# Half packs between score runs, finished input chunks as tile room, and seven instead of four quads with more VectorE exponentials

## The chip, the cores and the metric

The kernel runs on one core of a Trainium2 chip. The metric is the device time of one execution in microseconds (us). The runs of one call are repeated on one chip, and each call for a comparison times the kernel before as well. The profile's span is some 1.6 to 2.7 us shorter than the time of the same execution.

## The reference

Sequence 2048, width 512, 32 heads of 16. An attention branch and a gated bilinear branch on the same input are mixed by one sigmoid per row:

```python
g = _sigmoid((x * gate_w).sum(-1, keepdims=True))
a = _A_ref(x, A_wqkv, A_wo)      # softmax attention, 32 heads of 16
b = _B_ref(x, B_w_gate, B_w_up, B_w_down)   # (x Wg) * (x Wu), then Wd; F = 1376
return g * a + (1 - g) * b
```

The costly part is 32 heads x 2048 x 2048 exponentials.

## The kernel before

The Python program is a planner. It keeps a clock for each engine, and at each step decides what that engine issues next, from durations that are written into it. What comes out is a fixed order of instructions with semaphores; the chip then runs that order, at its own pace. So nearly every constant in the source changes the order and not an instruction.

The work is cut into 32 "quads" (4 row groups of the array, one chunk of 512 queries). Each quad has 64 score tiles of 128 x 512. TensorE makes up to four of them in one run. Their exponentials come in two ways:

```python
# ScalarE: two or three tiles (banks of PSUM) in one instruction
src = bass.AP(lo.tensor, lo.offset, [list(lo.ap[0]), [1, 512 * n]])
k = _Task("act", [sc] + old,
    lambda a: a.activation(cell_ap(c), src, ACT.Exp, scale=LN2 / 128.0),
    AOH + 0.4267 * n, ...)

# VectorE ("D" unit): integer arithmetic on the bits, one tile, then three shifted copies
lambda v: v.tensor_scalar(cell_ap(..., int16), bk.ap, CB, 0.0, ALU.add, ALU.max)
fn = lambda v: v.tensor_single_scalar(cell_ap(c, I16), cell_ap(src, I16), 32.0 * k, ALU.add)
# [the copies are shared between VectorE and GpSimd]
```

A ScalarE tile is used in one weighted product, a VectorE tile in four (itself and three copies, with weights scaled). 16 of the 64 tiles of a quad go to VectorE; in the quads listed in `HBQ` it is 20:

```python
HBQ = [16, 22, 24, 30]
UA0.append(UA0[-1] + (44 if m in HBQ else 48))   # tiles of ScalarE in a quad
```

Between score runs TensorE does the weighted products and the "fills", all other matrix products, in packs of 512 columns. A score run uses another tiling mode than these. The planner lets a pack go first only if the scores would still be in time:

```python
tN = act_need()          # when ScalarE will have emptied its queue
tL = tN - 0.62
...
if ua == 0 or (can and t + PACK > max(tE, tL) + 0.08):
    return False         # [wait for the score run: the pack does not fit]
```

If VectorE's tiles lag by more than `LC`, one is handed back to ScalarE (`convert()`).

The softmax here doesn't subtract the row's maximum and nothing guards it: scores larger than these inputs give would overflow.

## Time and profile before

| | before |
|---|---|
| median time | 712.44 us |
| first exponential starts, from the start of the span | 8.8 us |
| exponentials, first start to last end | 691.4 us |
| tail after the last exponential | 9.8 us |
| ScalarE tiles, in instructions | 1520, in 671 |
| VectorE tiles | 528 |

The prediction below shows the lines. In them, psS and psX are buffers in PSUM, the memory to which TensorE writes its results; PT, wv, wd, hT and xT hold finished exponentials (the last four are buffers whose first content nobody reads any more).

In the tables below, "bubbles" are the sum, over all exponentials, of what each ended later after the one before it than 0.490, 0.917 or 1.343 us (one, two or three tiles). The kernel before has 0.4 us of them.

### The profile page before, as it was taken

What the parts mean: (1) busy time and instruction counts of PE and PEld (TensorE: products, weight loads), DVE (VectorE), ACT (ScalarE), POOL (GpSimd) and SP (SyncE); (2) the same over time, 40 slices, a digit from 0 to 9 for tenths busy, and PEclk for the clock granted to TensorE, in tenths of its full rate; (3) what the DMA queues carried; (4) which work ended last, traced back from release to release, by engine and by line L of the source; (5) the groups of instructions that cost most, each with busy time, mean ns of one, the idle gap of its engine ahead of it and who ended that gap; (6) DMA issues with size and microseconds to landing.
All of it is one profiled execution on the core that took longest, in us unless ns stands there. A gap on an engine that the chain in (4) does not pass through costs nothing.

```text
span 710.0 us, 21364 instructions
## 1 busy us (share of the span) xinstructions
PE 688.3 (97%) x9127; PEld 188.7 (27%) x9127; DVE 644.5 (91%) x1231; ACT 696.6 (98%) x686; POOL 459.3 (65%) x481
## 2 busy tenths in 40 slices
PE   8999999999999999999999999999999999999997
PEld 3323332222222222222222222222222222222222
DVE  6998999999998999898999989999899999988897
ACT  6999999999999999999999999999999999999995
POOL 4787788746654566575577565556768866665863
PEclk9999999999999999999999999999999999999999
DMA  6800001000200000000001010000000001000001
GB/s 141 258 10 11 20 19 22 17 18 22 82 21 17 18 29 26 20 18 20 18 2 28 25 44 17 17 7 18 20 18 18 21 18 36 18 20 18 8 16 46
DMA packets 33055, 21.66 MB, mean 31 GB/s; under 512 B 20380, under 2 KB 27964, under 8 KB 32960
## 3 DMA queue, kind: packets, MB, share of 16 engines
q1 hardware_dynamic: 31632, 19.64, 9.5%
q8 instruction: 71, 1.16, 0.7%
q10 hardware_dynamic: 1328, 0.66, 0.4%
q14 instruction: 24, 0.20, 0.1%
HBM read 15.12 MB, written 2.36 MB: 25 GB/s over the span
## 4 chain that ended last, share of the span: by engine, by line
ACT 70%; PE 22%; DVE 3%; issue 3%; POOL 1%; DVEq 0%; POOLq 0%; ACTq 0%
ACT PT L1697 59%; PE psS L494 8%; PE psO L1226 6%; PE psX L563 5%; ACT wd L1697 5%; ACT wv L1697 4%; ACT hT L1697 2%; DVE PT L1083 1%; PE psS L563 1%; POOL PT L1164 1%; DVE PT L1161 1%; PE psX L494 1%; PE psO L1805 0%; DVE wk L898 0%; PE psS L1816 0%
## 5 line engine op out<-in xcount | busy, mean ns | idle before, releaser
L1697 ACT ACTIVATE PT<-psS 128x1024 bf16<-128x1024 f32 (+1 forms) x569 | 621.9, 1466 | 0.1
L1164 POOL TENSOR_SCALAR PT<-PT 128x1024 int16<-128x1024 int16 x233 | 250.5, 1084 | 134.9 <-DVE PT L1161 46.3
L494 PE MATMUL psS<-QM,KE 32*128 32x512 bf16 x1981 | 253.9, 375 | 11.4 <-ACT PT L1697 4.5
L1083 DVE TENSOR_SCALAR PT<-psS 128x512 int16<-128x512 f32 x349 | 237.2, 686 | 26.9 <-PE psS L494 24.0
L1226 PE MATMUL psO<-PT,VS 128*18 128x512 bf16 x1698 | 225.3, 381 | 1.0 <-DVE oraw L1255 1.0
L1226 PE MATMUL psO<-PT,VD 128*18 128x512 bf16 x1228 | 194.9, 381 | 0.0
L1024 PEld LDWEIGHTS <-KE 32*128 32x128 bf16 x2048 | 63.2, 91 | 278.2 <-issue 159.1
L1161 DVE TENSOR_SCALAR PT<-PT 128x1024 int16<-128x1024 int16 (+1 forms) x240 | 102.4, 455 | 1.0
L1164 POOL TENSOR_SCALAR PT<-wv 128x1024 int16<-128x1024 int16 x57 | 60.7, 1075 | 32.7 <-DVE wv L1083 14.0
L1226 PEld LDWEIGHTS psO<-PT,VS 128*18 128x18 bf16 x1698 | 53.5, 88 | 52.0 <-issue 35.5
L1697 ACT ACTIVATE wv<-psS 128x1024 bf16<-128x1024 f32 (+1 forms) x48 | 67.0, 1395 | 0.0
L563 PE MATMUL psX<-wd,hT 128*32 128x512 bf16 (+1 forms) x704 | 59.8, 386 | 0.0
L1226 PEld LDWEIGHTS psO<-PT,VD 128*18 128x18 bf16 x1228 | 46.4, 88 | 35.2 <-issue 24.5
L1083 DVE TENSOR_SCALAR wv<-psS 128x512 int16<-128x512 f32 x71 | 48.3, 687 | 7.0 <-PE psS L494 6.7
L563 PE MATMUL psX<-xT,wu 128*32 128x512 bf16 x688 | 53.8, 384 | 0.0
L563 PE MATMUL psX<-xT,wg 128*32 128x512 bf16 x688 | 53.6, 383 | 0.0
L1226 PE MATMUL psO<-wv,VS 128*18 128x512 bf16 x179 | 51.4, 381 | 0.0
L1697 ACT ACTIVATE wd<-psS 128x1024 bf16<-128x1024 f32 (+1 forms) x37 | 47.6, 1411 | 0.0
L1226 PE MATMUL psO<-wv,VD 128*18 128x512 bf16 x174 | 39.4, 381 | 0.2 <-ACT PT L1697 0.2
L1164 POOL TENSOR_SCALAR wv<-PT 128x1024 int16<-128x1024 int16 x23 | 24.9, 1082 | 22.4 <-PE psO L1226 9.0
L1083 DVE TENSOR_SCALAR PT<-psX 128x512 int16<-128x512 f32 x49 | 33.7, 688 | 5.7 <-PE psS L494 5.1
L837 DVE TENSOR_TENSOR hT<-psX,usb 128x512 bf16<-128x512 f32 (+1 forms) x44 | 30.1, 683 | 2.4 <-PE psX L563 1.7
(128 smaller groups left out, 715.8 us busy)
## 6 DMA issues: line engine op xcount, KB each, us to landing
rb<-rscr SPq DMA_DIRECT2D x31, 256.0 KB
out_dram<-ost SPq DMA_DIRECT2D x12, 128.0 KB, 1.7
wu<-in_B_w_up_dram SPq DMA_DIRECT2D x1, 1376.0 KB, 8.0
wg<-in_B_w_gate_dram SPq DMA_DIRECT2D x1, 1376.0 KB, 11.0
wd<-in_B_w_down_dram SPq DMA_DIRECT2D x1, 1280.0 KB, 6.0
OT<-OX SPq DMA_DIRECT2D x60, 16.0 KB, 1.8
wo<-in_A_wo_dram SPq DMA_DIRECT2D x1, 512.0 KB, 11.6
out_dram<-wk SPq DMA_DIRECT2D x4, 128.0 KB, 1.7
```

The costliest lines, as they stand in the source:

```text
L494: return e.add_instruction(mybir.InstMatmult(name=nc.get_next_instruction_name(), engine=mybir.EngineType.PE, ins=[e.lower_ap(rhs), e.lowe ...
L563: return e.matmul(out_ap[32 * q : 32 * q + w, :], lhs[:, 32 * q : 32 * q + w], rhs, start=s0, stop=s1, tile_position=(0, 32 * q), skip_gro ...
L837: lambda v: v.tensor_tensor(hT[0:w, f, :], bk.ap[0:w, :], usb[0:w, n % 2, :], ALU.mult),
L1024: r = e.ldweights(w, tile_position=pos)
L1083: lambda v: v.tensor_scalar(cell_ap(pr["cell"][i : i + 1], mybir.dt.int16), bk.ap, CB, 0.0, ALU.add, ALU.max),
L1161: fn = lambda v: v.tensor_single_scalar(cell_ap(c, I16), cell_ap(src, I16), 32.0 * k, ALU.add)
L1164: fn = lambda g: g.tensor_scalar(cell_ap(c, I16), cell_ap(src, I16), 32.0 * k, 1.0, ALU.add, ALU.mult)
L1226: r = e.matmul(psO[32 * j : 32 * j + VW, :], pv_stationary(m, kt, j, k), cell_ap((cell,)), start=s0, stop=s1, tile_position=(0, 32 * j), s ...
L1697: lambda a: a.activation(cell_ap(c), src, ACT.Exp, scale=LN2 / 128.0),
```

## The change

Its intent: to take more exponentials from ScalarE (seven quads for four), and to make room for the work that this gives TensorE, with fill packs that can be split in two and with room for tiles in parts of the input that nobody reads any more. Some twenty constants of the planner are changed with it. The core of the diff, with cuts marked:

```diff
-    HBQ = [16, 22, 24, 30]
+    HBQ = [6, 9, 14, 16, 22, 24, 30]
...
+        for i in range(16):
+            cells[C_X + i].need = 10**6 if i in XNO else 3 * NB + 1 + 2 * FT
...
-        groups = [(C_H, FT, EH), (C_D, FT, ED), (C_V, 4, 9999), (0, NMAIN, 9999)]
+        groups = [(C_H, FT, EH), (C_D, FT, ED), (C_X, 16, 9999), (C_V, 4, 9999), (0, NMAIN, 9999)]
...
+        HP = 1
+        HPK = 0.112
...
         def col(out_ap, lhs, rhs, s0, s1):
+            if hsel[0] is not None:
+                hs = slice(256 * hsel[0], 256 * hsel[0] + 256)
+                out_ap = out_ap[:, hs]
+                rhs = rhs[:, hs]
...
-            if ua == 0 or (can and t + PACK > max(tE, tL) + 0.08):
+            if ua == 0:
                 return False
+            if can and t + PACK > max(tE, tN - TL2) + TLS:
+                return half_pack(t, max(tE, tN - TL2) + TLS - HTL)
...
-        LC = 7
-        LDO = 8
+        LC = 5
+        LDO = 6
+        TLM = 0.62
+        TLS = 0.08
+        TL2 = 0.7
...
-        AOH = 0.057
+        AOH = 0.0635
[cut: F0, WP, GP, PB, KW, LAP, LAC, CPR, LA2, FB, NFD, QMW, RSV, and the switch costs SW, SWC, PCX]
```

More of the change, by code (lines that the diff above doesn't have):

```diff
@@ L213, in _build @@
     C_V = NMAIN
-    C_H = C_V + 4
+    C_X = C_V + 4
+    C_H = C_X + 16
     C_D = C_H + FT
@@ L410, in _build @@
         flex = [slots[0][2], slots[1][2], X]
+        XNO = (0, 4)
         cells = [_Cell() for _ in range(NCELL)]
-        for i in range(C_V, C_H):
+        for i in range(C_V, C_X):
             cells[i].need = NB * NCH
+        for i in range(16):
+            cells[C_X + i].need = 10**6 if i in XNO else 3 * NB + 1 + 2 * FT
         for i in range(C_H, C_D):
@@ L418, in cell_ap @@
         def cell_ap(c, dt=None):
-            for buf, lo in ((wd, C_D), (hT, C_H), (wv, C_V), (PT, 0)):
+            for buf, lo in ((wd, C_D), (hT, C_H), (xT, C_X), (wv, C_V), (PT, 0)):
                 if c[0] >= lo:
@@ L422, in cell_ap @@
             w = 512
-            base = buf[:, c[0] - lo, :]
+            base = buf[:, (c[0] - lo) // 4, (c[0] - lo) % 4 * 512 : (c[0] - lo) % 4 * 512 + 512] if buf is xT else buf[:, c[0] - lo, :]
             dims = [[1, 512]]
@@ L484, in _build @@
         LKD = -0.07
+        HP = 1
+        HPK = 0.112
+        HTL = 0.04
         LKP = 0.1
         QMP = 3.2
-        QMW = 0.3
+        QMW = 0.0
         PLAT = 0.44
-        SW = 0.11
+        SW = 0.1035
+        SWC = 0.0945
+        PCX = 0.005
         pe = {"mode": "c"}
@@ L508, in pe_run @@
         def pe_run(deps, fn, occ, mode, t, lat=None, cb=None, pre=None):
-            sw = SW if mode != pe["mode"] else 0.0
+            sw = (SW if mode == "r" else SWC) if mode != pe["mode"] else 0.0
+            if mode == "c" and occ == PACK:
+                occ += PCX
             pe["mode"] = mode
@@ L548, in __init__ @@
                 self.pdeps = None
+                self.h = 0
         def fready(f, t):
@@ L558, in xdep @@
             return xt_all if ch == 0 else [d_x[ch]]
+        hsel = [None]
         def col(out_ap, lhs, rhs, s0, s1):
+            if hsel[0] is not None:
+                hs = slice(256 * hsel[0], 256 * hsel[0] + 256)
+                out_ap = out_ap[:, hs]
+                rhs = rhs[:, hs]
             def fn(e, q):
@@ L1103, in even @@
         def even(c):
-            g = [sum(x >= lo for lo in (C_V, C_H, C_D)) for x in c]
+            g = [sum(x >= lo for lo in (C_V, C_X, C_H, C_D)) for x in c]
             return min(g) == max(g) and c[1] > c[0] and all(b - a == c[1] - c[0] for a, b in zip(c, c[1:]))
@@ L1321, in _build @@
         HWF = 0.2
-        GP = 200.0
+        GP = 190.0
         K3L = 190
@@ L1333, in _build @@
                 fills.append(f_q(0, b, pos) if kind == "q" else f_k(b, ch, pos) if kind == "k" else f_v(b, ch, pos))
-        F0 = 210.0
-        WP = 36.0
+        F0 = 220.0
+        WP = 28.0
         WL = 18.0
@@ L1407, in start_fill, with do_fill @@
             st["fill"] = f
-        def do_fill(t):
+        def do_fill(t, half=False):
             f = st["fill"]
             mk, occ, mode = f.packs[f.i]
-            deps = f.old + f.deps() if f.i == 0 else []
+            deps = f.old + f.deps() if f.i == 0 and not f.h else []
             if f.pdeps is not None:
                 deps = deps + f.pdeps[f.i]
-            k = pe_run(deps, mk(f.bank), occ, mode, t)
+            if half or f.h:
+                hsel[0] = f.h
+                occ = HPK
+            fn = mk(f.bank)
+            hsel[0] = None
+            k = pe_run(deps, fn, occ, mode, t)
+            if occ == HPK and not f.h:
+                f.h = 1
+                HN[0] += 1
+                return k
+            f.h = 0
             f.i += 1
@@ L1421, in do_fill @@
                 if f.name[0] == "v":
-                    for i in range(C_V, C_H):
+                    for i in range(C_V, C_X):
                         cells[i].readers.append(k)
+                ch = {"k": f.name[-1], "q": f.name[1:2], "g": f.name[1:2], "u": f.name[1:2], "v": str(int(f.name[-1]) // 2) if f.name[0] == "v" else ""}.get(f.name[0], "")
+                for i in range(16):
+                    if f.name == "gate" or ch == str(i % 4):
+                        cells[C_X + i].readers.append(k)
                 st["fill"] = None
@@ L1443, in _build @@
         LEAD = 5
-        PB = 0.45
+        PB = 0.4
         PK = 2
-        KW = 4.0
-        LAP = 0.12
-        LAC = 0.1
-        CPR = 3.5
-        LC = 7
-        LDO = 8
+        KW = 4.5
+        LAP = 0.08
+        LAC = 0.12
+        CPR = 3.1
+        LC = 5
[3 more added lines that the diff above has]
+        TL2 = 0.7
         MG = 0.15
@@ L1458, in _build @@
         LA1 = 1
-        LA2 = 99
+        LA2 = 3
         XF = -99
-        FB = 0
+        FB = 3
         SWE = 0
-        NFD = 20
-        AOH = 0.057
+        NFD = 24
+        AOH = 0.0635
         M4 = 1
@@ L1469, in _build @@
         DEV = 0.6
-        RSV = 0.5
+        RSV = 0.0
         RSC = 1.0
@@ L1512, in convert, with half_pack @@
             st["na"] += 1
+        HN = [0]
+        def half_pack(t, lim):
+            f = st["fill"]
+            if f is None or f.name[0] not in "kqudw" + ("g" if f.name != "gate" else "") or t + HPK > lim or not HP or st["ua"] < 20:
+                return False
+            do_fill(t, not f.h)
+            return True
         def pe_step():
@@ L1528, in pe_step @@
             tN = act_need()
-            tL = tN - 0.62
+            tL = tN - TLM
             if can and tE <= t + (SWE if pe["mode"] != "r" else 0.0):
@@ L1541, in pe_step @@
                             return True
-                    return False
+                    return half_pack(t, tL - MG + 0.1)
                 fw = fill_next(t) if st["fill"] is None else None
@@ L1618, in run_at @@
             if len(exps) < 2 and all(f is not None for f in fr):
-                return max(max(fr) + SEM, act_need() - 0.62 - MG)
+                return max(max(fr) + SEM, act_need() - TLM - MG)
             if not exps:
@@ L1940, in _build @@
         _build.end = max(clock.values())
+        _build.hn = HN[0]
         now("sp", [o_out[T - 1], o_out[T - 2]], lambda e: e.nop(), 0.1)
```

## The prediction

> **What bounds the kernel now.** I read the page first, then the groups of instructions by shape on ScalarE, the time order of ScalarE, the waits, the stretches of 100 us, and at last the time order of TensorE. The page alone does not decide it: TensorE, VectorE and ScalarE all stand above 90%.
>
> ```profile
> PE 688.3 (97%) x9127; PEld 188.7 (27%) x9127; DVE 644.5 (91%) x1231; ACT 696.6 (98%) x686; POOL 459.3 (65%) x481
> ACT 70%; PE 22%; DVE 3%; issue 3%; POOL 1%; DVEq 0%; POOLq 0%; ACTq 0%
> ```
>
> The groups by shape count the exponential tiles (128x512 each) that ScalarE makes, two or three to an instruction:
>
> ```profile
> L1697 ACT ACTIVATE PT<-psS 128x1024 bf16<-128x1024 f32 x405 | 444.8, 1343 | 0.1
> L1697 ACT ACTIVATE PT<-psS 128x1536 bf16<-128x1536 f32 x163 | 285.4, 1775 | 0.0
> L1697 ACT ACTIVATE wv<-psS 128x1024 bf16<-128x1024 f32 x43 | 58.1, 1352 | 0.0
> L1697 ACT ACTIVATE wd<-psS 128x1024 bf16<-128x1024 f32 x28 | 33.8, 1295 | 0.0
> L1697 ACT ACTIVATE hT<-psS 128x1024 bf16<-128x1024 f32 x15 | 17.5, 1251 | 0.2 <-PE psS L494 0.2
> ```
>
> With the three smaller rows of 1536 columns (9, 5, 2) and one of 512 these are 491 two-tile, 179 three-tile and 1 one-tile instructions: 671 instructions, 982 + 537 + 1 = 1520 tiles. The kernel has 2048 score tiles; the other 528 are exponentials by integer arithmetic on VectorE (its rows at L1083 sum to 528). 1520 is exactly 32 quads of 48 less 4 for each of the four listed quads, so no tile was handed back from VectorE to ScalarE.
>
> The durations of 1.34 and 1.78 us overlap, so they are not the price. The time order gives it:
>
> ```profile
> 174.19 1.79 ACT L1697 ACTIVATE PT<-psS 128x1536 bf16<-128x1536 f32 x1
> 175.54 1.36 ACT L1697 ACTIVATE wd<-psS 128x1024 bf16<-128x1024 f32 x1
> 176.46 1.36 ACT L1697 ACTIVATE PT<-psS 128x1024 bf16<-128x1024 f32 x1
> 177.38 1.78 ACT L1697 ACTIVATE wd<-psS 128x1536 bf16<-128x1536 f32 x1
> ...
> 694.71 5.46 ACT L1697 ACTIVATE PT<-psS 128x1024 bf16<-128x1024 f32 x5
> 702.64 0.28 ACT L1922 ACTIVATE oraw<-psS 128x128 f32<-128x128 f32 x1 [2.48 <-PE psS L563]
> ```
>
> End to end: 175.98, 176.90, 177.82, 179.16. A two-tile instruction takes 0.92 us, a three-tile one 1.34 us; in the records 0.917 and 1.343, almost without spread. So a tile costs 0.426 us and an instruction 0.065 us besides. Check: the first exponential ends at 9.81, and 9.81 + 490 x 0.917 + 179 x 1.343 + 0.49 = 700.1; the last line above ends at 700.17. From 8.8 to 700.2 us ScalarE has **no bubble at all**. The wait view agrees: the only wait before an exponential is the first one's 0.2 us. What is left is a head of 8.8 us and a tail of 9.8 us.
>
> TensorE at 97% is not the bound: its ends are modelled and its record runs on while it waits. In its time order a score run is followed by products and then a return to scores:
>
> ```profile
> 41.65 0.39 PE L1226 MATMUL psO<-PT,VD 128*18 128x512 bf16 x4
> 42.03 0.37 PE L494 MATMUL psS<-QM,KE 32*128 32x512 bf16 x2
> 42.33 0.40 PE L563 MATMUL psS<-xT,wk 128*32 128x512 bf16 x4
> 42.56 0.39 PE L1226 MATMUL psO<-PT,VD 128*18 128x512 bf16 x4
> 42.95 0.37 PE L494 MATMUL psS<-QM,KE 32*128 32x512 bf16 x2
> ```
>
> Pack to pack is 0.22 us, score to pack 0.30, pack to score 0.38 here (42.03 - 41.65). Over all 670 returns in the records the last step has a mean of 0.385 and a smallest regular value of 0.32. The difference, 0.065 x 670 = some 43 us, is time in which a whole pack of 512 columns did not fit. And scores are early: in half of the runs they start 0.05 us after ScalarE frees their banks, and end 0.49 us before ScalarE has to have them.
>
> **What the Trainium skill says.** "ScalarE: Activation LUTs", section What ACT_TABLE_LOAD costs: 0.833 ns a column, a fixed part, and back-to-back instructions overlap by some 93 ns. The slope agrees (0.426 us for 512 columns); what remains fixed here is 0.065 us. "TensorE: Matmul & The Clock Gate", Back-to-back issue gap: N/2.4 + 2.5 ns, which is 109 ns for 256 columns. This kernel already has such packs (V projections): 24 matmuls, four at a time, are on record for 0.84 us where four alone take 0.28, so (0.84 - 0.28)/5 = 0.112 us a pack. "TensorEngine Tiling (Array Packing)", Key Properties: changing the tiling mode drains the array. It agrees: both 0.30 and 0.32 exceed a 0.216 us pack by a change of mode.
>
> **The change, part by part.**
> (1) Seven listed quads, not four. Each moves four tiles from ScalarE to VectorE: 3 x 4 = 12 tiles, 1520 to 1508 and 528 to 540. On the path: -12 x 0.426 = **-5.1 us**. Beside it: VectorE gets 12 evacuations at 0.60 (7.2 us; 0.69 as recorded, 0.60 end to end) and 36 shifted copies, shared with GpSimd as before (some 19 tiles at 0.17 and 17 at 0.54, 3 and 9 us). VectorE idles 65 us and GpSimd 250 us of the span. TensorE gets 36 more weighted products (a VectorE tile takes four instead of one): 9 packs x 0.216 = 1.9 us. The new quads belong to the same two head blocks, so no table of weights grows.
> (2) Half packs. A fill pack may be split in two of 256 columns where the gap holds no whole one. Cost: 0.224 for 0.216 us of work, nothing on the path; gain: perhaps a hundred to two hundred of the gaps used, 11 to 22 us of the 43. It removes no work from ScalarE, so alone it is worth nothing here; it pays for (1).
> (3) Finished chunks of xT as 14 more tile cells, only after a chunk's last reader, so from about 40% of the span on. No exponential waits for a cell now, so worth 0 by itself.
> (4) New scheduling constants. Scores are allowed to come a little earlier (0.70 for 0.62), the assumed ScalarE overhead and switch costs are nearer to the measured ones: worth 0 where there are no bubbles. Score runs may take a VectorE tile also into the other slot's third bank: slightly more full runs, fewer and larger ScalarE instructions. I guess 4 fewer of 671, -0.3 us. Against that, the lag at which a VectorE tile is handed back is 5 for 7: each costs 0.43 us; I guess two, +0.9 us. Some first bubbles: +0.2 us, a guess.
> Sum: 712.4 - 5.1 - 0.3 + 0.9 + 0.2 = 708.1; head and tail as they are. Since the constants look chosen to make the new plan pay, I lean on fewer returned tiles and put **707.3 us**.
>
> **The rivals.**
> A. VectorE becomes the limit in the listed quads: tiles lag, are handed back, and most of the 12 return to ScalarE. For: 91% busy, more than 20 us of waits on scores that cannot be moved, a lower hand-back limit. Against: no hand-back before, 65 us idle. It would give 710 to 712.
> B. TensorE becomes late: half packs and 9 more packs push score runs past the moment at which ScalarE runs dry. For: starts of the runs are already up to 0.42 us behind the release. Against: a reserve of 0.49 us, and 43 us of gaps for 2 us of new work. With 0.1 us in each of 30 runs it takes back 3 us: 709 to 711; badly out of step it could pass 714.
> C. The half packs clear the backlog and shorten the tail (9.8 us), or the fuller runs save more instructions: 704.5 to 706. Against: the tail is a serial chain after the last product; its longest wait, 2.5 us on ScalarE, is for the last quad's sums, not backlog.
>
> **Range and chances.** Full transfer and small gains give 705; half of the tiles handed back or some bubbles give 710. 8 in 10: 704.8 to 710.6. Faster by 2% means below 698.1: 14 us, where the only term on the path is 5. Slower by 2% (726.6) needs a stall of a kind that the trace does not show. Chances: faster 0.02, within 2% 0.95, slower 0.03.
>
> **What would show it.** Right: ScalarE tiles sum to 1508 to 1512 and VectorE's L1083 rows to 540 or a little less; exponentials still 0.917 and 1.343 us apart without waits; the last one ends near 695; matmul rows of 256 columns for the fills, with more matmuls in all; pack-to-score gaps nearer to 0.32. Wrong: waits of ScalarE on L494 (rival B), 1515 tiles or more (A), or a tail much shorter than 9.8 us (C). It would be wrong altogether if the end moved by more than the count of ScalarE tiles explains.

## The result

The changed kernel takes 707.29 us (706.72 to 707.46, 4 runs) against 712.44 us (711.67 to 712.72, 4 runs): -5.15 us. The ratio is 0.9928, 95% interval 0.9911 to 0.9945. Here and below a ratio is the mean time of one kernel's runs over that of the other's in the same rounds, so it is not quite the ratio of the medians.

The page of the changed kernel, engines and chain:

```profile
PE 682.9 (97%) x9299; PEld 193.8 (27%) x9299; DVE 651.9 (92%) x1223; ACT 691.7 (98%) x685; POOL 499.6 (71%) x515
ACT 71%; PE 22%; DVE 4%; issue 2%; POOL 0%; DVEq 0%; ACTq 0%; POOLq 0%
```

Hardly a share has moved, and that is right: the bound is the same engine, only with less to do. Its groups by shape, the two-tile ones and the largest three-tile one:

```profile
L1744 ACT ACTIVATE PT<-psS 128x1024 bf16<-128x1024 f32 x350 | 384.1, 1298 | 0.1
L1744 ACT ACTIVATE PT<-psS 128x1536 bf16<-128x1536 f32 x152 | 257.6, 1727 | 0.0
L1744 ACT ACTIVATE wv<-psS 128x1024 bf16<-128x1024 f32 x51 | 65.3, 1280 | 0.1
L1744 ACT ACTIVATE xT<-psS 128x1024 bf16<-128x1024 f32 x49 | 62.6, 1293 | 0.0
L1744 ACT ACTIVATE wd<-psS 128x1024 bf16<-128x1024 f32 x33 | 38.0, 1235 | 0.0
L1744 ACT ACTIVATE hT<-psS 128x1024 bf16<-128x1024 f32 x17 | 19.8, 1206 | 0.2 <-PE psS L503 0.2
```

These are 500 two-tile instructions. With 169 of three tiles (152, and 7, 6, 3, 1 in rows not shown) and one of one tile they make 670 instructions and 1000 + 507 + 1 = 1508 tiles. None was handed back, and VectorE has 540 (the sum of its rows at L1102). The end in the time order of ScalarE:

```profile
692.51 1.77 ACT L1744 ACTIVATE PT<-psS 128x1536 bf16<-128x1536 f32 x1
693.84 2.27 ACT L1744 ACTIVATE xT<-psS 128x1536 bf16<-128x1536 f32 x2
698.05 0.28 ACT L1969 ACTIVATE oraw<-psS 128x128 f32<-128x128 f32 x1 [1.93 <-PE psS L582]
```

The last exponential ends at 693.84 + 2.27 = 696.11. The first one starts at 9.56, so this stretch is 686.6 us long, 4.8 us less than before. That is 12 x 0.426 + 1 x 0.065 = 5.2 us less work and 0.4 us more bubbles (0.7 for 0.4). The head was 0.8 us longer in this execution (over all profiled ones it lay between 8.5 and 9.6 us, whatever the kernel). The tail is 705.4 - 696.1 = 9.3 us, 0.5 us shorter.

The split packs are the matmul rows of 256 columns at L582. I show the two largest:

```profile
L582 PE MATMUL psX<-wd,hT 128*32 128x256 bf16 x136 | 9.8, 278 | 0.0
L582 PE MATMUL psX<-xT,wu 128*32 128x256 bf16 x40 | 2.9, 278 | 0.0
```

All such rows together hold 272 matmuls, eight to a split pack: **34 packs** were split, of more than 700.

So the sum came out. The prediction also said why the parts matter: the quads pay, the half packs make room for them. That is what the experiments test.

### The profile page after: what moved, and what is told of

It is laid out like the page before. It is cut to its first block, busy times and chain, and to the rows that moved or that the text cites. A ratio compares the mean times of both kernels' runs of the same rounds, so it can differ in the third digit from the quotient of the medians.

```text
span 705.4 us, 21702 instructions
## 1 busy us (share of the span) xinstructions
PE 682.9 (97%) x9299; PEld 193.8 (27%) x9299; DVE 651.9 (92%) x1223; ACT 691.7 (98%) x685; POOL 499.6 (71%) x515
## 4 chain that ended last, share of the span: by engine, by line
ACT 71%; PE 22%; DVE 4%; issue 2%; POOL 0%; DVEq 0%; ACTq 0%; POOLq 0%
ACT PT L1744 55%; PE psS L503 7%; ACT xT L1744 7%; PE psO L1245 6%; ACT wv L1744 5%; PE psX L582 5%; ACT wd L1744 2%; ACT hT L1744 2%; PE psS L582 1%; PE psX L503 1%; DVE PT L1102 1%; PE psS L693 1%; PE psX L693 1%; PE psO L1852 0%; DVE PT L1180 0%
## 5 line engine op out<-in xcount | busy, mean ns | idle before, releaser
L1744 ACT ACTIVATE PT<-psS 128x1024 bf16<-128x1024 f32 (+1 forms) x502 | 568.1, 1428 | 0.1
L1183 POOL TENSOR_SCALAR PT<-PT 128x1024 int16<-128x1024 int16 x183 | 198.4, 1094 | 82.3 <-DVE PT L1102 31.8
L1102 DVE TENSOR_SCALAR PT<-psS 128x512 int16<-128x512 f32 x292 | 197.4, 684 | 14.0 <-PE psS L503 11.7
L1744 ACT ACTIVATE xT<-psS 128x1024 bf16<-128x1024 f32 (+2 forms) x56 | 72.8, 1338 | 0.0
L1180 DVE TENSOR_SCALAR PT<-PT 128x1024 int16<-128x1024 int16 x141 | 66.9, 491 | 0.8 <-PE psO L1245 0.2
L1183 POOL TENSOR_SCALAR PT<-xT 128x1024 int16<-128x1024 int16 x46 | 50.3, 1099 | 24.0 <-DVE xT L1102 7.9
L1102 DVE TENSOR_SCALAR xT<-psS 128x512 int16<-128x512 f32 x76 | 51.6, 686 | 6.2 <-PE psS L503 5.9
L582 PE MATMUL psX<-wd,hT 128*32 128x512 bf16 (+3 forms) x784 | 55.9, 362 | 0.0
L582 PE MATMUL psX<-xT,wu 128*32 128x512 bf16 (+1 forms) x708 | 55.1, 378 | 0.3 <-DVE ost L917 0.3
L582 PE MATMUL psX<-xT,wg 128*32 128x512 bf16 (+1 forms) x696 | 54.3, 381 | 0.4 <-DVE KE L621 0.4
L1245 PE MATMUL psO<-xT,VS 128*18 128x512 bf16 x203 | 51.4, 381 | 0.7 <-DVE oraw L1274 0.4
L1245 PE MATMUL psO<-xT,VD 128*18 128x512 bf16 x242 | 51.1, 380 | 0.1
L1183 POOL TENSOR_SCALAR PT<-wv 128x1024 int16<-128x1024 int16 x34 | 36.8, 1089 | 9.1 <-DVE PT L1180 2.8
L1102 DVE TENSOR_SCALAR PT<-psX 128x512 int16<-128x512 f32 x52 | 35.7, 686 | 6.1 <-PE psS L503 5.5
```

What stands on the lines that cost most here:

```text
L582: return e.matmul(out_ap[32 * q : 32 * q + w, :], lhs[:, 32 * q : 32 * q + w], rhs, start=s0, stop=s1, tile_position=(0, 32 * q), skip_gro ...
L1102: lambda v: v.tensor_scalar(cell_ap(pr["cell"][i : i + 1], mybir.dt.int16), bk.ap, CB, 0.0, ALU.add, ALU.max),
L1183: fn = lambda g: g.tensor_scalar(cell_ap(c, I16), cell_ap(src, I16), 32.0 * k, 1.0, ALU.add, ALU.mult)
L1245: r = e.matmul(psO[32 * j : 32 * j + VW, :], pv_stationary(m, kt, j, k), cell_ap((cell,)), start=s0, stop=s1, tile_position=(0, 32 * j), s ...
```

## The experiments

Two kinds are told apart. In one the order of the instructions is left as it is and the length of some work is changed. In the other the planner makes a new order, and then everything moves. "Replanned" marks the second kind. One table for all; tiles, instructions, bubbles and tail are from the profiled execution of each.

| run | time (median) | ratio to before | ScalarE tiles in instructions | bubbles | tail |
|---|---|---|---|---|---|
| before | 712.44 | 1 | 1520 in 671 | 0.4 | 9.8 |
| changed | 707.29 | 0.9928 | 1508 in 670 | 0.7 | 9.3 |
| b_cut12 | 708.06 | 0.9944 | 1508 in 671 | 1.8 | 9.8 |
| b_pe44 | 712.74 | 1.0011 | 1520 in 671 | 0.6 | 9.8 |
| a_cut24 | 701.30 | 0.9845 | 1484 in 670 | 5.7 | 9.3 |
| a_pe44 | 707.36 | 0.9932 | 1508 in 670 | 1.5 | 9.2 |
| a_whole34 | 707.04 | 0.9923 | 1508 in 670 | 1.3 | 9.2 |
| a_no_half (replanned) | 730.91 | 1.0264 | 1510 in 712 | 4.3 | 26.5 |
| a_no_half_tuned (replanned) | 708.81 | 0.9951 | 1508 in 658 | 4.0 | 9.1 |
| a_no_cells (replanned) | 708.47 | 0.9948 | 1508 in 672 | 1.2 | 10.7 |
| a_four (replanned) | 714.05 | 1.0029 | 1520 in 659 | 3.6 | 9.4 |
| b_six (replanned) | 717.41 | 1.0067 | 1512 in 689 | 0.6 | 17.4 |
| nine (replanned) | 704.41 | 0.9891 | 1500 in 666 | 2.8 | 9.0 |
| nine_no_half (replanned) | 707.13 | 0.9929 | 1500 in 668 | 7.5 | 9.1 |

Not all of these bubbles come from the order. In five of the runs the trace shows TensorE's granted clock at 0.5 for some microseconds while exponentials are still being made (`--windows`, column PEclk). In the other nine it is below 1 only after the last exponential.

| run | half clock, us from the start of the span | bubbles there or within about 1 us after | all bubbles | mean clock, all executions |
|---|---|---|---|---|
| a_cut24 | 678.7-682.1 | 1.1 | 5.7 | 0.997 in the profiled one, 1.0 in three |
| a_no_half_tuned | 677.8-684.7, 691.5-694.9 | 2.4 | 4.0 | 0.991-0.995 |
| a_four | 668.4-671.8, 685.4-692.2 | 2.7 | 3.6 | 0.990-0.993 |
| nine | 676.7-683.5 | 1.1 | 2.8 | 0.994-0.995 |
| nine_no_half | 319.8-326.6, 678.2-688.4 | 4.0 | 7.5 | 0.986-0.998 |

In the 3.4 us before each of these stretches TensorE was busy for only 43% to 65% of the time by its record. The changed kernel has 3.4 us at 60% near 682 us and kept its clock, so no limit can be read from this. No run tests what brings the clock down; where a conclusion below leans on one of these five runs, it says so.

The theory at the start (P): ScalarE is the only bound, its tiles set the time, and TensorE has dead time to spare. The rival (Q): TensorE is as full as ScalarE.

### 1. Less work on ScalarE, order untouched

```diff
+            co = c
+            if n == 2 and st["ua"] > 300:
+                CUT[0] += 1
+                if CUT[0] % 20 == 0 and CUT[1] < 12:    # a_cut24: % 10, < 24
+                    CUT[1] += 1
+                    co = c[:1]
-            src = bass.AP(..., [1, 512 * n]])
+            src = bass.AP(..., [1, 512 * len(co)]])
-                lambda a: a.activation(cell_ap(c), src, ...)
+                lambda a: a.activation(cell_ap(co), src, ...)
```

> The kernel before, its order untouched; after the 300th tile, every 20th two-tile exponential, 12 in all, works on one tile only (result wrong on purpose). ScalarE alone gets 12 x 0.426 = 5.1 us less to do, and TensorE and VectorE exactly the same work. Theory P (ScalarE is the only bound, TensorE has spare gaps): 707.3 us, within 0.7. Rival Q (TensorE is as full as ScalarE): less than half of it arrives, 710 us or more, with a longer tail after the last exponential.

> The changed kernel, order untouched, 24 of its two-tile exponentials after the 300th tile cut to one tile (wrong on purpose): ScalarE 10.2 us less, all else the same. Theory P: 697.1 us, and no waits of ScalarE. Rival Q: TensorE cannot follow, 702 us or more, with waits of ScalarE for scores or a longer tail.

Measured: 708.06 us for b_cut12, -4.05 us against the runs of before on the same chip (712.11), four fifths of the 5.1 us. The cut instructions are in the profile of b_cut12, groups by shape, as one-tile rows (one of the 13 was there before):

```profile
L1705 ACT ACTIVATE PT<-psS 128x512 bf16<-128x512 f32 x11 | 9.7, 878 | 0.0
L1705 ACT ACTIVATE wv<-psS 128x512 bf16<-128x512 f32 x2 | 1.8, 903 | 0.0
```

Missing is what the bubbles take: 1.8 us for 0.4. The 24 cuts in the changed kernel brought 707.29 - 701.30 = 6.0 us of 10.2 (24 x 0.426), and here the bubbles are 5.7 us for 0.7. Both results are wrong on purpose (relative errors of 0.040 and 0.048).

What follows: ScalarE's tiles do set the time, nearly one for one at first. But the return falls, from 79% for twelve to 59% for twenty-four. Neither P (all of it) nor Q (less than half) holds as it was put. The trace of b_cut12 shows where the rest went: a bubble of 0.08 to 0.09 us follows directly on each of the 12 cuts. One of them, first ScalarE, then TensorE:

```profile
176.10 1.36 ACT L1705 ACTIVATE wd<-psS 128x1024 bf16<-128x1024 f32 x1
177.01 0.94 ACT L1705 ACTIVATE PT<-psS 128x512 bf16<-128x512 f32 x1
177.93 1.45 ACT L1705 ACTIVATE wd<-psS 128x1536 bf16<-128x1536 f32 x1
```

```profile
177.51 0.38 PE L494 MATMUL psS<-QM,KE 32*128 32x512 bf16 x3
```

The exponential before the cut one ends at 177.46 and frees its banks. The next score run starts 0.05 us later, as soon as any in the kernel before (0.05 us at the least), and its own exponential ends at 179.38: 0.52 us more than its 1.343 us after the scores' start. So 0.57 us pass for this hand-over, and the cut exponential covers only 0.49 us of them. TensorE is not late there. In a_cut24 19 of the 24 cuts look the same; at the other five the score run starts 0.07 to 0.27 us after the release, and the bubble is 0.11 to 0.32 us. The bubbles directly after the cuts sum to 1.0 us in b_cut12 and 2.7 us in a_cut24; 1.1 us more in a_cut24 lie at its half clock. So most of what b_cut12 lost is a limit of the cut itself, one tile being shorter than the hand-over, and it does not speak for Q.

### 2. More work on TensorE, order untouched

```diff
-                    lambda bk, kt=kt: col(bk.ap, wu[...], xT[...], kt == 0, kt == KD - 1),
+                    lambda bk, kt=kt: twice(col(bk.ap, wu[...], xT[...], kt == 0, kt == KD - 1), kt == 0),
```

`twice` issues the pack two times; the second one starts the sum again, so the result is right.

> The changed kernel, order untouched; the first pack of each of the 44 up projections is issued twice (the result stays right): TensorE gets 44 packs of 0.216 us, 9.5 us, that the planner did not count. Theory P: they fall into TensorE's dead time before score runs, 707.3 to 708.5 us. Rival Q: TensorE has no reserve, 712 to 717 us.

> The kernel before with the same 44 uncounted packs, 9.5 us of TensorE work. Theory P: 712.4 to 713.5 us. Rival Q: 717 to 722 us. If it takes them better than the changed kernel does, the half packs and the three quads have used up part of TensorE's reserve.

The pages of b_pe44 and of a_pe44 show the 172 added matmuls (44 packs, four of them of three matmuls), 9127 to 9299 and 9299 to 9471:

```profile
PE 692.5 (97%) x9299; PEld 193.5 (27%) x9299; DVE 643.0 (90%) x1231; ACT 697.0 (98%) x686; POOL 459.5 (65%) x481
```

```profile
PE 684.9 (97%) x9471; PEld 197.8 (28%) x9471; DVE 651.8 (92%) x1223; ACT 692.1 (98%) x685; POOL 498.1 (71%) x515
```

Measured: +0.6 us before (712.74 against 712.11 on the same chip) and +0.1 us in the changed kernel (707.36 against 707.29), for 9.5 us of work each. As P said: TensorE absorbs this. The dead time is there, and it is usable: a whole pack to a score run takes 0.32 us at least, and what is above that sums to some 44 us before and some 32 us in the changed kernel. In the traces with the added packs these sums are 34 and 22 us: the packs went into the gaps. The Trainium skill, "Perfetto Trace Analysis", section Identifying the Most-Contended Engine, says that matmul busy time is not a good measure of how close a kernel is to the roofline. These runs agree: the changed kernel's TensorE is 97% busy by its page, and took 9.5 us more work for 0.1 us.

### 3. The half packs, made whole in place

Here the order is kept, but each split pack is issued whole where its first half stood, and nothing where its second half stood:

```diff
-            if half or f.h:
-                hsel[0] = f.h
-                occ = HPK
-            fn = mk(f.bank)
+            if half or f.h:
+                occ = HPK          # the planner still counts a half
+            fn = mk(f.bank)
+            if occ == HPK and f.h:
+                [no instruction; the clock advances as before]
```

> The changed kernel in its own order, but each of the 34 split packs is issued whole where its first half stood, and nothing where its second half stood. The score run after the first half comes up to 0.11 us later than planned, the one after the second half earlier. Theory T (TensorE has time there, as the 44 extra packs showed; the half packs only matter to the planner, which refuses to let a score run be that late): 707.0 to 707.8 us. Rival H (the halves save time on the chip): up to 34 x 0.11 = 3.7 us, 709 to 711 us, with waits of ScalarE at these places.

The page of a_whole34 has 136 matmuls fewer, 4 for each of the 34:

```profile
PE 681.8 (97%) x9163; PEld 189.9 (27%) x9163; DVE 651.6 (92%) x1223; ACT 691.9 (98%) x685; POOL 499.4 (71%) x515
```

Measured: 707.04 us (706.53 to 708.01), ratio to before 0.9923 where the changed kernel has 0.9928. Theory T holds: on the chip the half packs save no time that these runs can tell. All 34 gaps that the planner found too short for a whole pack took one (and the place of each second half became free), bubbles are 1.3 us for 0.7, and the end did not move.

### 4. The planner without half packs

```diff
-        HP = 1
+        HP = 0
```

> The changed kernel with the half packs switched off, all else the same; its order is planned anew and comes to 712 ScalarE instructions for 1510 tiles (670 for 1508 in the changed kernel). Theory P' (the half packs only fill time that TensorE has anyway; ScalarE's tiles set the end): the 42 more instructions cost 42 x 0.065 = 2.7 us and two tiles 0.9 us, so 711 us at most. Rival Q' (half packs are what lets TensorE keep pace with seven quads): TensorE falls behind, ScalarE ends below 705 us all the same and a tail of products longer than 20 us follows: 725 to 735 us.

Measured: 730.91 us, +2.6% on before. ScalarE has 1510 tiles and ends its exponentials at 702.4 us, and then TensorE works through products that were left over. In the waits of a_no_half it shows as one line, ScalarE waiting for the last quad's sums:

```profile
ACT oraw L1969 <- PE psS L582: 18.7, 1, 18.7
```

In TensorE's groups for the stretch from 703 us on, 176 of the matmuls are down projections; the last score run starts at 701.7 us. So rival Q' is what this run shows: a backlog. But it is not the lack of 34 split packs as such that makes it, since experiment 3 took them away at no cost. The new order has 712 score runs with an exponential, for 670. A run costs two changes of mode: 0.30 us to the next pack and 0.32 us back, less the 0.22 us that a pack takes anyhow, makes 0.40 us. 42 more are an estimated 17 us of TensorE time. The dead time before runs is some 47 us, for 32. Together these are more than the 23.6 us by which the kernel became longer. Why the planner chose smaller runs is not visible in a trace; that part stays open.

Is it the half packs or the set of constants around them? In the next run half packs stay off and constants are searched again with the planner's own clock (WP 20, F1 1450, LEAD 6, CPR 3.5, TL2 0.62, XF -20, NFD 18, NP 6; HTL has no effect here).

> Half packs off, seven quads and xT tiles kept, with eight scheduling constants searched again for this case (658 ScalarE instructions, 1508 tiles). Theory P': 706.5 to 708 us, as fewer instructions give 0.8 us back. Rival Q': without half packs TensorE delivers scores late, ScalarE waits some 7 us in sum, 710 to 713 us: the gain of the change is gone though 12 tiles have left ScalarE.

Measured: 708.81 us (708.45 to 708.98), between the two bands. The tail is back to 9.1 us with 658 instructions, and bubbles are 4.0 us. So without half packs, a search finds an order that keeps seven quads and most of the gain, 1.5 us behind the changed kernel. What half packs bring is 23.6 us if one switches them off in a plan made for them, and at most 1.5 us if one plans again; "at most", because the search was short, and because 2.4 of the 4.0 us of bubbles lie at stretches of half clock that the changed kernel does not have.

### 5. The room in finished input chunks

```diff
-            cells[C_X + i].need = 10**6 if i in XNO else 3 * NB + 1 + 2 * FT
+            cells[C_X + i].need = 10**6
```

> The changed kernel without the tiles in finished xT chunks (1508 tiles, 672 instructions). Theory P: worth nothing, 707 to 708 us, for no exponential waited for a tile before. Rival R (room for tiles lets VectorE's four copies be held until TensorE takes them): some 2 us, 709 to 710 us.

Measured: 708.47 us (708.15 to 708.99), 1.2 us over the changed kernel and between the bands of P (707 to 708) and R (709 to 710). The spans of the profiles differ by 1.7 us: 1.4 us is in the tail (10.7 for 9.3 us), 0.5 us in bubbles and 0.1 us in two more instructions; a shorter head takes 0.3 us back. The intervals of the two ratios overlap (0.9936 to 0.9961 and 0.9911 to 0.9945), while the single times do not (708.15 us and more, 707.46 us and less): it seems to be worth something of that order in this plan. Whether that is the room itself or the order that came with it, one run does not tell.

### 6. The quads alone, and all but the quads

```diff
# a_four: the changed kernel
-    HBQ = [6, 9, 14, 16, 22, 24, 30]
+    HBQ = [16, 22, 24, 30]
# b_six: the kernel before
-    HBQ = [16, 22, 24, 30]
+    HBQ = [9, 14, 16, 22, 24, 30]
```

With all seven quads, the kernel before gets an order in which ScalarE and TensorE may meet in one PSUM bank, so six were run.

> The changed kernel with the four listed quads of before: 1520 tiles in 659 instructions on ScalarE. Theory P: +12 x 0.426 - 11 x 0.065 = +4.4 us, 711.7 us. Rival S (the gain comes from the fuller packing and the constants, not from the quads): 709 us or less.

> The kernel before with six listed quads instead of four and nothing else (with seven its new order fails the race check): 1512 tiles in 689 ScalarE instructions, from 1520 in 671. Theory P (ScalarE's tiles and instructions set the end): -8 x 0.426 + 18 x 0.065 = -2.2 us, 710.1 us. Rival Q'' (more and smaller score runs fill TensorE, which then ends with a backlog of fill products, as in the run without half packs): ScalarE's last exponential moves to about 698, but the tail grows from 9.8 to 15 us or more, 714 to 719 us.

a_four: 714.05 us, +6.8 us on the changed kernel, where 4.4 us were expected. The difference of tiles and instructions is as forecast; the rest is bubbles, 3.6 us for 0.7, and 2.7 us of them lie at two stretches of half clock. Rival S (709 us or less) falls: all of the change but the quads gives no gain. That it is even 1.7 us slower than before (712.30 on the same chip) can't be laid on its order alone: all five executions have a mean clock of 0.990 to 0.993, those of before 0.998 to 1.0, and without these 2.7 us it would be at an estimated 711.4 us, near theory P's 711.7.

b_six: 717.41 us, +5.1 us, though ScalarE has eight tiles fewer and ends at 698.1 us, 2.0 us earlier than before. From the time order of the tail of b_six, first TensorE, then ScalarE:

```profile
699.17 0.39 PE L1226 MATMUL psO<-PT,VD 128*18 128x512 bf16 x3
699.39 6.44 PE L563 MATMUL psS<-wd,hT 96*32 96x512 bf16 x116
705.66 0.23 PE L563 MATMUL psS<-usb,sel 128*32 128x128 bf16 x4
```

```profile
706.43 0.28 ACT L1922 ACTIVATE oraw<-psS 128x128 f32<-128x128 f32 x1 [8.29 <-PE psS L563]
```

After the last weighted product, 116 matmuls of down projections come in a row, 6.4 us. The tail is 17.4 us for 9.8. This is rival Q'', and it corrects theory P: TensorE has dead time, yet in this order it could not use it, and what it could not place came after the end of ScalarE's work. 18 more runs at 0.40 us and 24 more products (6 packs at 0.22) are an estimated 8.5 us of added TensorE work, and dead time fell only by some 3 us; the difference is about what was lost.

So neither half of the change gains its part alone: two of the three quads in the kernel before cost 5.1 us, all but the quads brings nothing (+1.7 us, with the half clock in it), and both together gain 5.15 us.

### 7. A version that is faster than both

If the planner refuses room that the chip has, what does it assume wrongly? Where an exponential did wait for its scores, its end minus the start of the score run, less its own 0.426 us a tile and 0.065 us, was nearly always 0.52 to 0.54 us in b_cut12, a_cut24 and a_pe44. The planner adds 0.71 us (0.44 for the matmul, 0.06 for the semaphore, 0.21 until the end is seen). (At the half clock it was 0.75 to 0.76 us for 13 of 17 late exponentials in the five runs of the table above.) I took 0.15 us off for this one wait, and searched constants and lists of quads again:

```diff
-            if sc.end + SEM > t:
+            if sc.end + SEM - AEA > t:          # AEA = 0.15
-            t0 = max(clock["act"], exps[0][2].end + SEM)
+            t0 = max(clock["act"], exps[0][2].end + SEM - AEA)
-    HBQ = [6, 9, 14, 16, 22, 24, 30]
+    HBQ = [6, 9, 14, 16, 17, 22, 24, 25, 30]
-        TLM = 0.62
+        TLM = 0.5
-        TL2 = 0.7
+        TL2 = 0.55
[cut: HTL 0.0, GP 200, F0 200, WP 40, F1 1455, SEED 12, LEAD 6, KW 5.0, LAP 0.06, LAC 0.08, LC 7, KP 0.6, FBL 20]
```

> Nine listed quads. In the runs so far a score run that is too late delays ScalarE only when it starts less than 0.53 us plus the tiles' own time before the planned end of its exponential; the planner allows for 0.71 us. Here the planner is told 0.15 us less, and its constants are searched again: 1500 tiles in 666 ScalarE instructions. Theory T (ScalarE's count sets the end as long as the planner can place TensorE's packs, and the planner was what refused them): 707.3 - 8 x 0.426 - 4 x 0.065 = 703.6 us, between 702.5 and 704.5, without waits of ScalarE beyond 1.5 us in sum. Rival (the allowance was needed): score runs come late, bubbles of 0.1 to 0.2 us in many places, 706 us or more.

Measured: **704.41 us** (704.34 to 704.98), ratio to before 0.9891, and the result is right. It is 2.9 us faster than the changed kernel. No run changes the allowance alone: the list of quads and fifteen constants differ too, so how much of the 2.9 us it brought is not shown. The page of it:

```profile
PE 673.3 (96%) x9386; PEld 200.6 (29%) x9386; DVE 653.3 (93%) x1230; ACT 689.0 (98%) x681; POOL 508.2 (72%) x524
```

1500 tiles in 666 instructions, exponentials over at 693.6 us, a tail of 9.0 us. The dead time before score runs is down to some 19 us. The time is within the band, the bubbles (2.8 us) are above the 1.5 us that I had allowed. Two of the largest are near the end. First TensorE's score run, then ScalarE, from the time order:

```profile
684.05 0.38 PE L1245 MATMUL psO<-PT,VD 128*18 128x512 bf16 x1
684.37 0.39 PE L503 MATMUL psS<-QM,KE 32*128 32x512 bf16 x3
```

```profile
683.01 1.45 ACT L1745 ACTIVATE PT<-psS 128x1536 bf16<-128x1536 f32 x1 [0.48 <-PE psS L503]
684.80 1.45 ACT L1745 ACTIVATE PT<-psS 128x1536 bf16<-128x1536 f32 x1 [0.34 <-PE psS L503]
```

The run starts at 684.37 and its matmuls end at 684.76; the exponential starts at 684.80 and ends at 686.25. That is 1.88 us from the start of the scores, 0.54 us more than the 1.343 us of three tiles: the figure above, at a place where ScalarE stands and waits. But why the scores came late is in the clock. The stretches just before, engine by engine, with the granted clock third from the end:

```profile
670.00:676.70 6.70, 4.24 (x50) 1.19 (x50) 5.42 (x10) 6.70 (x7) 5.67 (x6) 1.00 0.05 20
676.70:683.50 6.80, 6.27 (x50) 1.22 (x54) 5.58 (x12) 6.32 (x6) 4.41 (x5) 0.50 0.05 11
```

First TensorE (the first busy time) is at work for 4.24 of 6.70 us. Then its clock is at half; packs follow each other there at 0.39 to 0.42 us where 0.22 is the rule, and the exponential at 683.01 ends 0.76 us plus its own time after the start of its scores at 682.36. So these two bubbles (0.6 and 0.45 us) do not show that an order at full clock is too tight.

The last run asks whether half packs are needed for nine quads:

```diff
-        HP = 1
+        HP = 0
[cut: HTL 0.02, WP 20, SEED 40, PB 0.45, LAP 0.1, NF 16, NP 10, FBL 15, against the run "nine"]
```

> The same with the half packs switched off and eight constants searched again: 1500 tiles in 668 instructions. Theory T: 707.3 - 3.4 - 0.1 = 703.8 us, within 1 us: half packs are not needed for it. Rival (half packs carry the additional quads): a backlog of fill products in the tail, 706 us or more.

Measured: 707.13 us, but from 705.78 to 709.22, by far the widest spread of all. There is no backlog (tail 9.1 us), so the rival's mechanism is not what happened; but neither did 703.8 us come. In the profiled execution (709.22 us, the slowest) bubbles are 7.5 us, and 4.0 us of them lie at two stretches of half clock, 17.0 us long together. The second slowest execution (708.26 us) has the second lowest mean clock (0.990 after 0.986); the other four, at 0.995 to 0.998, took 705.78 to 707.89 us. So part of the spread goes with the clock. Whether the half packs keep "nine" steadier, or its constants do, stays open.

## Why the prediction was right

The number was met: 707.3 forecast, 707.29 measured. Point by point:

- **ScalarE as the bound, at 0.426 us a tile.** Shown. Taking tiles away without touching the order brought four fifths of their time, and adding 9.5 us to TensorE cost 0.6 us at most. One word was too strong: "no bubble at all" is 0.4 us. (The check sum before it comes to 700.0, not 700.1.)
- **Part 1, the quads, -5.1 us.** Right in count (1508 and 540) and in size (the stretch of exponentials shrank by 4.8 us). For GpSimd the split was wrong: I shared the new copies as before, 17 tiles. In fact GpSimd makes 402 pair copies for 368 (its rows at L1183), 68 tiles more, and VectorE makes 816 copies for 848. GpSimd's busy time rose by 40 us for an estimated 9. It cost nothing, as GpSimd is not on the path.
- **Part 2, the half packs.** "Alone it is worth nothing here; it pays for (1)" is borne out in its first half, as far as a_four shows, and wrong in mechanism. I guessed one to two hundred split packs and 11 to 22 us of dead time used; there are 34, at most 4 us. And they do not pay with time on the chip: made whole, they cost nothing. What they change is what the planner will place, and that was worth at most 1.5 us once it planned without them (a_no_half_tuned). That they pay for the quads is more than was shown.
- **Part 3, the xT tiles, 0.** Measured at 1.2 us, in a new order; small, and neither shown to be zero nor clear of it. The tiles came in earlier than said, too: the first is written at 226 us, a third of the span, not 40%.
- **Part 4, the constants.** Two returned tiles were guessed, none came (-0.9 us). Four fewer instructions were guessed, one came (+0.2 us). Bubbles grew by 0.4 us for a guessed 0.2. The leaning from 708.1 to 707.3 went the right way, and the unforeseen 0.5 us of a shorter tail does the rest. So the exact hit owes something to luck; the term of 5.1 us does not.
- **Rival A** did not occur. **Rival C** occurred in a small part (the tail, 0.5 us).
- **Rival B** was put too narrowly. I spoke of late scores and bubbles, and put against it "43 us of gaps for 2 us of new work". For the changed kernel that holds, though the "reserve of 0.49 us" was too large: it counted to the modelled end of the matmuls. With the hand-over of 0.52 to 0.54 us, a score run 0.05 us after the release leaves an estimated 0.917 - 0.05 - 0.53 = 0.34 us. But b_six and a_no_half show the form in which TensorE really becomes the bound: ScalarE runs on undisturbed, and the unplaced products wait in the tail. A sum of gaps was not proof that an order can use them.

## What to carry to other kernels

Where a fixed order is made from a model of durations, ask of each gap whether the chip or only the model refuses to fill it: keep the order, put a longer instruction in, and look. Judge a part of such a change only with its order made anew for it; here two of the three new quads alone lost 5.1 us, and the whole gained 5.15 us, because a new order moves everything. Read the granted clock by stretches before a bubble is laid on the order: a mean of 0.993 hid 10 us at half clock. A backlog on an engine that is not the bound does not show as waits along the way, but as a longer tail after the bound engine's last work.

## What the Trainium skill lacked or had wrong

- "ScalarE: Activation LUTs", section What ACT_TABLE_LOAD costs: an instruction with immediate scale and bias takes a fixed 186 ns, and back-to-back ones overlap by about 93 ns, which leaves an estimated 93 ns. Here exponentials from PSUM come every 917 and 1343 ns for 1024 and 1536 columns: the slope agrees, and 65 ns are left besides.
- "TensorEngine Tiling (Array Packing)", section Key Properties, says that changing the tiling mode drains TensorE, with no figure. Here it is 0.30 us from a score run to the next pack and 0.32 us back, where packs of one mode follow each other at 0.22 us: some 0.08 and 0.10 us for the two changes.
- "TensorE: Matmul & The Clock Gate", section Back-to-back issue gap, agrees for 256 columns (109 ns by its formula, 0.112 us here). What no page that I read gives is the whole hand-over from TensorE to ScalarE: here the exponential ends 0.52 to 0.54 us plus its own time after the score run's start, where the planner counts 0.71 us. What that difference costs, no run shows by itself.
